# Attention scores in two-bank PSUM tiles, with one tanh and one exp for two heads

## The chip, the cores and the metric

The kernel runs on one core of one Trainium2 chip. The metric is the device time of one execution in microseconds (us), as the median of several runs. The five engines are TensorE (PE, with its weight loads as PEld), VectorE (DVE), ScalarE (ACT), GpSimd (POOL) and SyncE (SP), which issues most of the transfers. PSUM, into which TensorE writes, has eight banks of 512 float32 values per partition.

## What is computed

The reference is attention with capped scores, followed by a layer norm, a feed-forward block and a residual:

```python
scores = (1 / np.sqrt(64)) * np.matmul(q, k.transpose(0, 1, 3, 2))   # batch 4, 12 heads, 448 tokens, 64 wide
scores = cap * np.tanh(scores / cap)                                 # cap = 30
scores = scores - np.max(scores, axis=-1, keepdims=True)
attn = np.exp(scores)
attn = attn / (np.sum(attn, axis=-1, keepdims=True) + 1e-09)
x = np.matmul(attn, v)             # heads joined to (4, 448, 768)
xn = (x - mean) / np.sqrt(var + 1e-06) * g_ln
out = x + np.maximum(xn @ w_ch1, 0.0) @ w_ch2                        # 768 -> 3072 -> 768
```

All is float32; w_ch1 and w_ch2 arrive as float64. Since tanh bounds the scores by the cap, the kernel leaves out the maximum and lets the exponent's sums run as they are. (A second program for other caps, `general`, lies beside it and does not run here.)

## The kernel before

There are 48 heads (4 batches of 12). They are worked in quads: four heads, as two pairs p = 0, 1, with k = 0, 1 for the head of a pair. Keys are cut into three blocks of 128 (j = 0, 1, 2) and a leftover of 64. For a pair and a block, TensorE multiplies keys with queries for both heads (line 639; the two heads sit on the two halves of the partitions and are issued alternately), into two tiles of one PSUM bank each. ScalarE evacuates each bank with a tanh of 448 elements (line 684) into the tile `e`, and after three blocks raises a head's 3 x 448 values with one exp (line 688). The leftover keys of the quad's four heads share two more banks (line 666), two tanh and one exp of 2 x 448 (line 696). Then TensorE multiplies with v (line 480, leftover line 487) into two output banks `o`; VectorE adds up the key blocks (lines 503 and 505), TensorE sums them over partitions (lines 562 and 566) into one bank `s`; outputs and sums are copied out of PSUM (lines 535 and 537), transposed (lines 588 and 602, banks `f`) and divided (line 612).

Beside this, while heads 0 to 23 run, VectorE and GpSimd convert the first weights from float64 (lines 859 to 867, split in two at lines 420 and 423), and layer norms of the first token tiles follow (lines 769 to 819). The feed-forward block in two parts fills the rest of the time: lines 930 to 964 first, with the remaining heads spread between, and from about 500 us lines 1139 to 1231 for the other token tiles.

The order of all this is not written by hand. Each operation is added with an engine, a cost in ns and a due time; `Order.emit` plays a list scheduler over these costs, and each engine's queue gets its instructions in the order in which that scheduler started them. On the chip each queue runs in that order and waits where it must. A place in PSUM is handed out by the scheduler: kind `bank` has eight places, and a tag has a limit of its own (`zf`, the scores of heads 0 to 23, six banks; `z`, later scores, four; `o` two; `s` one; `f` six). A place that comes free goes to the end of the list and the first of the list is taken. `fits` refuses an operation whose places aren't free, and the scheduler goes on to the next operation by due time. `realize` makes one tile per bank. Names that the steps touch: `quad` (line 433 chooses `zf` or `z`), `products` (the score matmuls), `scores` with `into` (tanh and exp), `TAGS`, `Order.add`, `Order.emit`, `realize`.

Of the kernel before, what the change touches and what calls it, by code (L numbers as in the profile page):

```python
# [32 lines left out]
WRAP = 4  # L33
LEAD = 24
SPLIT = 28
SLOTS = 8
# [56 lines left out]
TAGS = dict(  # L93
    z=('bank', 4), zf=('bank', 6), o=('bank', 2), s=('bank', 1), f=('bank', 6), kq=('d', 4), v=('v', 3), s1=('d', 2), er=('d', 2),
    e=('e', 3), e2=('e', 2), kh=('k', 2), kl=('k', 2), ot=('b', 4), ss=('b', 1), stage=('a', 3),
# [14 lines left out]
class Buf:  # L110


    def __init__(self, pool, kind, tag, shape, dtype):
        self.pool, self.kind, self.tag, self.shape, self.dtype = pool, kind, tag, shape, dtype
        self.users, self.ap, self.last, self.share, self.since = 0, None, 0.0, None, 0.0


# [19 lines left out]
class Order:  # L137
# [4 lines left out]
    def __init__(self, places, limits):  # L142
        self.places, self.limits = places, limits
        self.ops, self.writer, self.readers, self.taken, self.dead = [], {}, {}, [], set()

    def add(self, engines, fn, reads=(), writes=(), allocs=(), due=0.0, dma=0, after=(), lag=0.0):
# [29 lines left out]

    def emit(self, realize):
        free = {e: 0.0 for e in "SGVATP"}
# [15 lines left out]
        def fits(o):  # L194
            if o.wait and not slots[o.wait[0]] and o.wait[1].ap is None:
                return False
            need = {}
            for b in o.bufs:
                if b.ap is None:
                    for k in keys(b):  # L200
                        need[k] = n = need.get(k, 0) + 1
                        if len(slots[k]) < n:
                            o.wait = k, b
                            return False
            return True

        while pending:
            done = False
            for e in free:
# [25 lines left out]
                for b in o.bufs:  # L235
                    b.users -= 1
                    b.last = max(b.last, o.end)
                    if b.share:
                        b.share.last = max(b.share.last, b.last)
                        b.share.users -= not b.users  # L240
                        if not b.users and not b.share.users:
                            for at in b.share.at:
                                heappush(due_back, (b.share.last + CROSS, *at))
                    elif not b.users:
                        for k, at in zip(keys(b), b.at):
                            heappush(due_back, (b.last + CROSS, k, at))
# [99 lines left out]
class Program:  # L346
    def __init__(self, tc, general, ahead, kq, v, w1, w2, out):
# [8 lines left out]
        self.order = Order(self.places, self.limits)  # L356
        self.given, self.grown = {}, {}
        if not general:
# [33 lines left out]
    def realize(self, b, at):  # L392
        key = (b.pool, b.kind, at)
        if key not in self.tiles:
            self.tiles[key] = self.pools[self.grown.get(key, b.pool)].tile([128, self.sizes[b.pool, b.kind]], F32, bufs=1, name=f"{b.kind}{at}")
# [9 lines left out]
        return ap  # L405

    def eng(self, e):
# [18 lines left out]
    def quad(self, i, at):  # L426
# [5 lines left out]

        self.zs = "zf" if i < FIRST else "z"
        kqs = []
# [138 lines left out]
    def finish(self, i, pairs, ps, due, late):  # L573
# [23 lines left out]
        for j, tl, p in self.token_tiles(b):  # L597
# [17 lines left out]
            if tl >= NA:  # L615
# [4 lines left out]
                    reads=writes, writes=[("xd", tl, (h0, p.start))], due=due, dma=128 * W * 4)  # L620

    def products(self, kqs, l, r, due, into, allocs, at_once):

# [18 lines left out]
        for n in range(0, len(slots), at_once):  # L642
            now = slots[n:n + at_once]
            zs = [[self.buf("ps", self.zs, [128, 512], F32) for _ in range(2)] for _ in now]

            def qk(e, now=now, zs=zs):
                for (p, j), z in zip(now, zs):
                    for both in zip(*(mul(z[k].ap[:, :S], p, k, j) for k in range(2))):
                        for one in both:
                            one()  # L650
# [3 lines left out]
            self.add({"T": 200 + len(now) * cost}, qk, reads=[x for p in ps for x in sources(p)],  # L654
                     writes=[z for zz in zs for z in zz], allocs=[allocs[p] for p in ps], due=due[now[0][0]] - PLAN["qk"])
            for (p, j), z in zip(now, zs):
                for k in range(2):
                    into(p, k, j, z[k])

        def rest(cost=0, then=None, reads=(), writes=()):  # L660
            zs = [self.buf("ps", self.zs, [128, 512], F32) for _ in range(2)]

            def qk(e):
                for p, kq in enumerate(kqs):
                    for k, z in enumerate(zs):
                        self.nc.tensor.matmul(z.ap[p * REST:p * REST + REST, :S], lhsT=kq.ap[rows[k], l, 128 * NK:],
                                              rhs=kq.ap[rows[k], r], start=True, stop=True)
# [5 lines left out]
            for k, z in enumerate(zs):  # L673
                into(2, k, 0, z)

        return rest

    def scores(self, es, er, kqs, due, at_once):
        nc, add = self.nc, self.add
        tiles = [*es, er]  # L680
        parts = lambda p, k: [(tiles[p], k, j) for j in range(NK if p < 2 else 1)]
# [12 lines left out]
        def finish(*a):  # L694
            rest(*a)
            add({"A": ACTS(2 * S) + 93}, lambda e: nc.scalar.activation(er.ap, er.ap, AF.Exp, scale=self.capt),
                reads=parts(2, 0) + parts(2, 1), writes=[er], due=due[2])

        return finish

    def scores_general(self, es, er, kqs, due, at_once):
# [6 lines left out]

        def into(p, k, j, z):
            add({"A": ACTP(S) + 93}, lambda e: nc.scalar.activation(  # L710
                tiles[p].ap[:, k, j] if p < 2 else tr.ap[:, k], z.ap[:, :S], AF.Tanh, scale=self.sc),
                reads=[z], writes=[tiles[p]], due=due[p])

# [601 lines left out]

    def close(self, *names):
        for n in names:
            self.cms.pop(n).__exit__(None, None, None)
# [4 lines left out]
    def run(self):  # L1323
# [13 lines left out]
        self.open("xna", side="right")  # L1337
        self.open("ps", 1, PSUM)

        A0, ASTEP, BSTEP = PLAN["start"], PLAN["step"], PLAN["bstep"]  # L1340
# [58 lines left out]
        self.planned = self.order.emit(self.realize)  # L1399
        self.close("ps", "wd", "hc", "xo2", "xo1", "y", "xC", "xd", "small")  # L1400
# [53 lines left out]
```

## Time and profile before

| | |
|---|---|
| median of 3 runs | 872.41 us (872.37 to 874.22) |
| the profiled execution, own time | 872.27 us |
| its span, first to last instruction | 870.5 us |
| granted TensorE clock, mean | 0.997 |
| PE busy | 850.3 us (98%) |
| DVE busy | 701.3 us (81%) |
| ACT busy | 523.8 us (60%) |
| POOL busy | 162.4 us (19%) |

The profile is one execution, and 1.8 us of its time lie outside the span. Busy times are unions of an engine's records. Matmul records are pipelined and each float32 matmul shows as two records, so a mean per record is longer than its share of the queue; where a duration matters, it is better read from one start to the next. "issue" in the chain of waits is time in which an engine waited for nothing that the profile shows. The wide picture of the span in 40 slices is of little use here, since a slice is 22 us long; tables by stage are of more.

### The profile page before, as it was taken

How to read it: one execution, taken by the hardware profiler on the slowest of the kernel's cores; microseconds unless marked ns; L12 is line 12 of the kernel's file. 1: busy time of each engine (PE TensorE's matmuls, PEld its weight loads, DVE VectorE, ACT ScalarE, POOL GpSimd, SP SyncE). 2: the span in 40 equal slices, each digit the busy share in tenths (PEclk: the TensorE clock that was granted, in tenths of full speed). 3: DMA queues.
4: the chain of work that ended last, by engine and by line, in shares of the span. 5: the costliest groups of instructions: out<-in, count | busy, mean ns of one | idle time of the engine just before them, and what ended most of it. 6: DMA issues, size and time to landing. Idle time of an engine off the chain costs nothing.

```text
span 870.5 us, 12961 instructions
## 1 busy us (share of the span) xinstructions
PE 850.3 (98%) x4718; PEld 705.6 (81%) x4718; DVE 701.3 (81%) x1154; ACT 523.8 (60%) x860; POOL 162.4 (19%) x206
## 2 busy tenths in 40 slices
PE   8899999999999999999999999999999999999995
PEld 4344477979889799799799988989998999898984
DVE  2996597888789779687689978887888788878884
ACT  7889848645654646445436545665666566656750
POOL 1430041211122111111110002223122312231121
PEclk9999999999999999999999999999999999999998
DMA  9996527566676675654563245787879787968697
GB/s 233 237 265 169 140 69 228 164 216 172 181 218 194 198 211 158 192 177 114 179 237 110 73 164 109 162 164 142 181 157 174 132 182 161 177 124 186 129 180 188
DMA packets 55003, 148.97 MB, mean 171 GB/s; under 512 B 7312, under 2 KB 19088, under 8 KB 54928
## 3 DMA queue, kind: packets, MB, share of 16 engines
q1 hardware_dynamic: 41680, 111.86, 43.1%
q0 software_dynamic: 13248, 36.18, 25.0%
q8 instruction: 39, 0.64, 0.3%
q14 instruction: 36, 0.29, 0.1%
HBM read 85.88 MB, written 62.13 MB: 170 GB/s over the span
## 4 chain that ended last, share of the span: by engine, by line
PE 86%; DVE 5%; DMA 2%; ACT 2%; issue 1%; POOL 1%; SPq 0%; DVEq 0%; POOLq 0%
PE bank L1139 7%; PE bank L1142 7%; PE bank L1140 7%; PE bank L1219 6%; PE bank L1221 6%; PE bank L1220 6%; PE bank L959 6%; PE bank L930 6%; PE bank L961 5%; PE bank L960 5%; PE bank L932 5%; PE bank L931 5%; PE bank L480 5%; PE bank L639 4%; PE bank L602 1%; PE bank L562 1%
## 5 line engine op out<-in xcount | busy, mean ns | idle before, releaser
L1236 POOL DMA_DIRECT2D out_dram<-x x92 | 80.5, 1000 | 333.1 <-ACT x L1227 209.1
L1227 ACT ACTIVATE x<-bank 128x384 f32<-128x384 f32 x184 | 87.6, 488 | 38.7 <-PE bank L1221 32.4
L1139 PE MATMUL bank<-X,q 128*128 128x512 f32 x252 | 100.0, 397 | 2.0 <-ACT y L1151 1.9
L1231 DVE TENSOR_TENSOR x<-bank,x 128x384 f32<-128x384 f32 x141 | 75.9, 553 | 30.8 <-PE bank L1221 24.5
L930 PE MATMUL bank<-hA,q 128*128 128x384 f32 x288 | 100.1, 348 | 0.1
L684 ACT ACTIVATE e<-bank,sc 128x448 f32<-128x448 f32 x144 | 81.7, 666 | 30.4 <-PE bank L639 30.2
L1140 PE MATMUL bank<-X,q 128*128 128x512 f32 x252 | 99.5, 395 | 0.0
L1142 PE MATMUL bank<-X,q 128*128 128x512 f32 x252 | 99.4, 395 | 0.0
L959 PE MATMUL bank<-w,hh 128*128 128x384 f32 x288 | 98.4, 342 | 0.0
L1219 PE MATMUL bank<-w,hop 128*128 128x384 f32 x288 | 97.4, 338 | 0.6 <-DVE x L1231 0.3
L932 PE MATMUL bank<-hA,q 128*128 128x384 f32 x288 | 97.6, 339 | 0.3 <-DVE q L423 0.3
L931 PE MATMUL bank<-lA,q 128*128 128x384 f32 x288 | 97.5, 338 | 0.0
L961 PE MATMUL bank<-w,hl 128*128 128x384 f32 x288 | 97.2, 338 | 0.0
L960 PE MATMUL bank<-w,hh 128*128 128x384 f32 x288 | 97.2, 337 | 0.0
L1221 PE MATMUL bank<-w,hop 128*128 128x384 f32 x288 | 96.9, 337 | 0.0
L1220 PE MATMUL bank<-w,hop 128*128 128x384 f32 x288 | 96.8, 336 | 0.0
L862 POOL TENSOR_SCALAR raw<-raw 128x768 f32<-128x768 f32 x48 | 54.5, 1138 | 225.5 <-ACT c L858 209.2
L964 DVE TENSOR_TENSOR x<-bank,x 128x384 f32<-128x384 f32 x144 | 75.7, 547 | 11.7 <-PE bank L961 11.3
L688 ACT ACTIVATE e<-e,capt 128x1344 f32<-128x1344 f32 x48 | 66.6, 1456 | 0.0
L480 PE MATMUL bank<-e,v 128*64 128x448 f32 x288 | 60.7, 547 | 1.9 <-ACT d L684 1.0
L930 PEld LDWEIGHTS bank<-hA,q 128*128 128x128 f32 x288 | 54.0, 188 | 9.0 <-issue 5.5
L416 ACT ACTIVATE w<-c 128x768 fp32r<-128x768 f32 x33 | 27.9, 845 | 54.5 <-DVE c L867 23.6
(162 smaller groups left out, 1823.5 us busy)
## 6 DMA issues: line engine op xcount, KB each, us to landing
raw<-in_w_dram SPq DMA_DIRECT2D x48, 768.0 KB, 5.1
out_dram<-x POOLq DMA_DIRECT2D x92, 384.0 KB, 7.4
kept<-c SPq DMA_DIRECT2D x47, 384.0 KB, 5.6
d<-in_kq_dram SPq DMA_DIRECT2D x48, 224.0 KB, 6.3
d<-kept SPq DMA_DIRECT2D x24, 384.0 KB, 5.1
c<-kept SPq DMA_DIRECT2D x23, 384.0 KB, 3.5
v<-in_v_dram SPq DMA_DIRECT2D x24, 227.5 KB, 5.7
v<-in_v_dram SPq DMA_DIRECT2D x24, 195.0 KB, 6.0
```

The lines of the kernel that those rows point to most:

```text
L930: nc.tensor.matmul(ps.ap[:, :n], lhsT=w1h.ap[:, wc], rhs=xh.ap[:, c], start=(c == 0), stop=False)
L931: nc.tensor.matmul(ps.ap[:, :n], lhsT=w1h.ap[:, wc], rhs=xl.ap[:, c], start=False, stop=False)
L932: nc.tensor.matmul(ps.ap[:, :n], lhsT=w1l.ap[:, wc], rhs=xh.ap[:, c], start=False, stop=(c == CC - 1))
L959: nc.tensor.matmul(o, lhsT=h[0].ap[:, mc], rhs=w[0].ap[:, hc], start=(f == 0), stop=False)
L960: nc.tensor.matmul(o, lhsT=h[0].ap[:, mc], rhs=w[1].ap[:, hc], start=False, stop=False)
L961: nc.tensor.matmul(o, lhsT=h[1].ap[:, mc], rhs=w[0].ap[:, hc], start=False, stop=(f == last))
L1139: nc.tensor.matmul(ps.ap, lhsT=wh.ap[:, wc], rhs=xs[c].ap[:, 0], start=start and c == 0, **o)
L1140: nc.tensor.matmul(ps.ap, lhsT=wh.ap[:, wc], rhs=xs[c].ap[:, 1], start=False, **o)
L1142: nc.tensor.matmul(ps.ap, lhsT=wl.ap[:, wc], rhs=xs[c].ap[:, 0], start=False, **o)
L1219: nc.tensor.matmul(o, lhsT=hh.ap[:, mc], rhs=wh.ap, start=start, stop=False, **skip)
L1220: nc.tensor.matmul(o, lhsT=hh.ap[:, mc], rhs=wl.ap, start=False, stop=False, **skip)
L1221: nc.tensor.matmul(o, lhsT=hl.ap[:, mc], rhs=wh.ap, start=False, stop=True, **skip)
```

## The change

Four aligned two-bank tiles are made at the start and cover PSUM. Everything that took one bank takes a half of such a tile. The scores of heads 0 to 23 take a whole one: the two heads of a pair (or the two banks of leftover keys) stand in its two halves, one tanh reads both (2 x 448 elements), and one exp raises the two heads' 2 x 3 x 448 values. The costs given to the scheduler are 1000 for such a tanh and twice the former cost for such an exp. Heads 24 to 47 keep single banks, tanh of 448 and exp of 1344.

The scheduler's `take` gives a wide buffer a pair of places that are both free, and gives a single bank, as long as wide buffers are still to come, first a place whose partner is taken. Since one tile now has two banks whose users have nothing to do with one another, `emitted` declares for each instruction on PE, DVE and ACT that it needs no order against the last 40 accesses of the tile's other bank by another engine, unless they share something else, or the instruction touches a tile for the first time after a pool was closed.

```diff
+PAST = 40
+TANH, EXP = 1000, ACTS(NK * S) + 93
-    z=('bank', 4), zf=('bank', 6), o=('bank', 2), s=('bank', 1), f=('bank', 6), ...
+    z=('bank', 4), zf=('bank', 3), o=('bank', 2), s=('bank', 1), f=('bank', 6), ...
...
         for b in op.bufs:
+            self.wide += b.wide and not b.users
...
+    def take(self, slots, b, kind):
+
+        if kind != "bank":
+            return [slots.pop(0)] if slots else None
+        if b.wide:
+            at = next((at for at in slots if not at % 2 and at + 1 in slots), None)
+            if at is None:
+                return None
+            slots.remove(at)
+            slots.remove(at + 1)
+            return [at, at + 1]
+        if not slots:
+            return None
+        at = min(slots, key=lambda at: (at ^ 1 in slots and self.wide > 0, slots.index(at)))
+        slots.remove(at)
+        return [at]
...
-                        need[k] = n = need.get(k, 0) + 1
-                        if len(slots[k]) < n:
+                        if k not in left:
+                            left[k] = list(slots[k])
+                        if not self.take(left[k], b, None if k[0] else k[2]):
                             o.wait = k, b
...
-                        b.at = [slots[k].pop(0) for k in keys(b)]
-                        b.ap = realize(b, b.at[0])
-                o.fn(e)
+                        b.at = [(k, at) for k in keys(b) for at in self.take(slots[k], b, None if k[0] else k[2])]
+                        b.ap = realize(b, b.at[0][1])
+                        self.wide -= b.wide
+                run(o, e)
...
+        if b.kind == "bank":
+            two = self.tiles["ps", "two", at // 2]
+            if b.wide:
+                return two.rearrange("p (k n) -> p k n", k=2)[:, :, :S]
+            self.tiles[key] = two[:, at % 2 * 512:at % 2 * 512 + 512]
...
+    def emitted(self, op, e):
...
+        for x in block.instructions[n:]:
+            reads, writes = (list(self.regions(side)) for side in (x.ins, x.outs))
+            names = {t for t, _, _ in reads + writes}
+            fresh = self.reused and names - self.seen
+            self.seen |= names
+            banks = {(t, k) for t, lo, hi in reads + writes if t in self.pairs for k in range(2) if lo < 512 * k + 512 and hi > 512 * k}
+            for t, k in banks:
+                other = t, 1 - k
+                if other not in banks and not fresh:
+                    for y, before, after in self.recent.get(other, ()):
+                        if x.engine != y.engine and not (meet(writes, before + after) or meet(reads, after)):
+                            self.tc.declare_no_dep(x, y, reason="another bank of the tile")
+                past = self.recent.setdefault((t, k), [])
+                past.append((x, reads, writes))
+                del past[:-PAST]
...
+    def scored(self):
+        if self.zs == "z":
+            return [self.buf("ps", "z", [128, 512], F32) for _ in range(2)]
+        z = self.buf("ps", "zf", [128, 2, 512], F32)
+        z.wide = True
+        return [z]
...
-        def into(p, k, j, z):
-            add({"A": ACTP(S) + 93}, lambda e: nc.scalar.activation(
-                tiles[p].ap[:, k, j] if p < 2 else er.ap[:, k], z.ap[:, :S], AF.Tanh, scale=self.sc),
-                reads=[z], writes=[(tiles[p], k, j)], due=due[p])
-            if p < 2 and j == NK - 1:
-                add({"A": ACTS(NK * S) + 93}, lambda e: nc.scalar.activation(
-                    tiles[p].ap[:, k], tiles[p].ap[:, k], AF.Exp, scale=self.capt),
-                    reads=parts(p, k), writes=[(tiles[p], k)], due=due[p])
+        both = slice(0, 2)
+
+        def into(p, j, zs):
+            for k, z, ks in [(k, z, [k]) for k, z in enumerate(zs)] if len(zs) == 2 else [(both, *zs, [0, 1])]:
+                add({"A": TANH if len(ks) == 2 else ACTP(S) + 93}, lambda e, k=k, z=z: nc.scalar.activation(
+                    tiles[p].ap[:, k, j] if p < 2 else er.ap[:, k], z.ap if len(z.shape) > 2 else z.ap[:, :S], AF.Tanh, scale=self.sc),
+                    reads=[z], writes=[(tiles[p], x, j) for x in ks], due=due[p])
+                if p < 2 and j == NK - 1:
+                    add({"A": EXP * len(ks)}, lambda e, k=k: nc.scalar.activation(
+                        tiles[p].ap[:, k], tiles[p].ap[:, k], AF.Exp, scale=self.capt),
+                        reads=[(tiles[p], x, j) for j in range(NK) for x in ks], writes=[(tiles[p], x) for x in ks], due=due[p])
...
     def close(self, *names):
+        self.reused = True
...
+        for i in range(4):
+            self.tiles["ps", "two", i] = self.pools["ps"].tile([128, 1024], F32, bufs=1, name=f"two{i}")
```

## Rows read from the trace of the kernel before

**Rows 1.** Busy us, share of the span and instructions of three engines.
```profile
PE 850.3 (98%) x4718; PEld 705.6 (81%) x4718; DVE 701.3 (81%) x1154; ACT 523.8 (60%) x860; POOL 162.4 (19%) x206
```

**Rows 2.** Busy us by stage; columns in the first line.
```profile
core 0: us, PE busy (x) PEld busy (x) DVE busy (x) ACT busy (x) POOL busy (x), PEclk, DMA share, GB/s
0.00:10.00 10.00, 8.70 (x41) 6.91 (x42) 1.35 (x11) 4.89 (x9) 1.50 (x15) 1.00 0.75 162
0.00:110.00 110.00, 103.18 (x611) 44.89 (x612) 73.94 (x139) 94.35 (x138) 22.62 (x50) 1.00 0.79 209
200.00:300.00 100.00, 100.00 (x590) 88.70 (x590) 82.04 (x124) 57.51 (x81) 18.45 (x17) 1.00 0.64 187
30.00:40.00 10.00, 8.82 (x44) 2.94 (x44) 9.97 (x17) 8.02 (x12) 2.75 (x4) 1.00 1.05 279
12.00:32.00 20.00, 17.18 (x101) 6.53 (x102) 13.59 (x16) 19.81 (x29) 5.69 (x8) 1.00 0.93 261
62.00:74.00 12.00, 10.99 (x72) 5.08 (x70) 8.19 (x20) 11.81 (x17) 0.88 (x1) 1.00 1.00 270
74.00:106.00 32.00, 31.42 (x204) 11.92 (x200) 18.89 (x36) 29.04 (x47) 1.02 (x7) 1.00 0.46 121
```

**Rows 3.** The chain of waits, 12 to 107 us: start us, us, what.
```profile
12.16 7.29 DMA raw<-in_w_dram
...
35.04 1.46 DVE d L503
...
62.20 1.14 ACT e L684 x2
...
68.46 2.63 ACT e L684 x5
...
72.22 1.47 ACT e L688
...
74.19 0.63 DVE lA L819
...
106.18 1.15 ACT e L684 x2
```

**Rows 4.** Waits, 10 to 110 us: us in total, times, longest us.
```profile
ACT e L684 <- PE bank L639: 7.8, 7, 2.1
...
PEld bank L480 <- ACT e L688: 3.6, 4, 1.3
```

**Rows 5.** The tanh group, 0 to 130 us: busy us, mean ns, idle before.
```profile
L684 ACT ACTIVATE e<-bank,sc 128x448 f32<-128x448 f32 x82 | 46.7, 688 | 12.1 <-PE bank L639 12.1
```

**Rows 6.** ScalarE in order of time, 70 to 90 us: start us, us.
```profile
70.91 2.77 ACT L688 ACTIVATE e<-e,capt 128x1344 f32<-128x1344 f32 x2
73.53 3.00 ACT L815 ACTIVATE hA<-bank,gt 128x384 fp32r<-128x384 f32 x6
...
77.58 3.39 ACT L684 ACTIVATE e<-bank,sc 128x448 f32<-128x448 f32 x6
80.68 2.90 ACT L688 ACTIVATE e<-e,capt 128x1344 f32<-128x1344 f32 x2
...
85.48 1.05 ACT L696 ACTIVATE d<-d,capt 128x896 f32<-128x896 f32 x1
86.41 2.75 ACT L684 ACTIVATE e<-bank,sc 128x448 f32<-128x448 f32 x5
```

**Rows 7.** All engines in order of time, 24 to 28 us: start us, us.
```profile
24.18 2.53 PE L639 MATMUL bank<-d 64*128 64x448 f32 x12
...
25.71 3.39 ACT L684 ACTIVATE e<-bank,sc 128x448 f32<-128x448 f32 x6
...
27.59 1.14 DVE L537 COPY b<-bank 128x448 f32<-128x448 f32 x2
```

More of the change, by code (lines that the diff above doesn't have):

```diff
@@ L93 @@
 TAGS = dict(
-    z=('bank', 4), zf=('bank', 6), o=('bank', 2), s=('bank', 1), f=('bank', 6), kq=('d', 4), v=('v', 3), s1=('d', 2), er=('d', 2),
+    z=('bank', 4), zf=('bank', 3), o=('bank', 2), s=('bank', 1), f=('bank', 6), kq=('d', 4), v=('v', 3), s1=('d', 2), er=('d', 2),
     e=('e', 3), e2=('e', 2), kh=('k', 2), kl=('k', 2), ot=('b', 4), ss=('b', 1), stage=('a', 3),
@@ L115, in __init__ @@
         self.users, self.ap, self.last, self.share, self.since = 0, None, 0.0, None, 0.0
+        self.wide, self.at = False, ()
 class Part:
@@ L144, in __init__ @@
         self.ops, self.writer, self.readers, self.taken, self.dead = [], {}, {}, [], set()
+        self.wide = 0
     def add(self, engines, fn, reads=(), writes=(), allocs=(), due=0.0, dma=0, after=(), lag=0.0):
@@ L175, in drop, with emit @@
             self.slots[kind].remove(at)
-    def emit(self, realize):
+    def take(self, slots, b, kind):
[13 more added lines that the diff above has]
+        return [at]
+    def emit(self, realize, run):
         free = {e: 0.0 for e in "SGVATP"}
@@ L196, in fits @@
                 return False
-            need = {}
+            left = {}
             for b in o.bufs:
@@ L244, in emit @@
                     elif not b.users:
-                        for k, at in zip(keys(b), b.at):
+                        for k, at in b.at:
                             heappush(due_back, (b.last + CROSS, k, at))
@@ L356, in __init__ @@
         self.order = Order(self.places, self.limits)
-        self.given, self.grown = {}, {}
+        self.given, self.grown, self.seen, self.recent, self.reused = {}, {}, set(), {}, False
         if not general:
@@ L405, in realize, with regions @@
         return ap
+    def regions(self, side):
+        for a in side:
+            ap = getattr(a, "bass_ap", None)
+            if ap is not None:
+                (pitch, _), *dims = ap.ap
+                lo = ap.offset % pitch
+                yield ap.tensor.name, lo, lo + 1 + sum(d * (n - 1) for d, n in dims)
+    def emitted(self, op, e):
+        block = self.nc.cur_bb.bb
+        n = len(block.instructions)
+        op.fn(e)
+        if self.general or e not in "TVA":
+            return
+        meet = lambda one, two: any(a[0] == b[0] and a[1] < b[2] and b[1] < a[2] for a in one for b in two)
+        for x in block.instructions[n:]:
[13 more added lines that the diff above has]
+                del past[:-PAST]
     def eng(self, e):
@@ L431, in quad @@
         part = HEADS[i // H]
-        self.zs = "zf" if i < FIRST else "z"
+        self.zs = "zf" if i < FIRST and not self.general else "z"
         kqs = []
@@ L620, in finish, with score @@
                     reads=writes, writes=[("xd", tl, (h0, p.start))], due=due, dma=128 * W * 4)
+    def scored(self):
[4 more added lines that the diff above has]
+        return [z]
+    def score(self, z, k):
+        return z[0].ap[:, k, :S] if len(z) == 1 else z[k].ap[:, :S]
     def products(self, kqs, l, r, due, into, allocs, at_once):
@@ L643, in products @@
             now = slots[n:n + at_once]
-            zs = [[self.buf("ps", self.zs, [128, 512], F32) for _ in range(2)] for _ in now]
+            zs = [self.scored() for _ in now]
             def qk(e, now=now, zs=zs):
                 for (p, j), z in zip(now, zs):
-                    for both in zip(*(mul(z[k].ap[:, :S], p, k, j) for k in range(2))):
+                    for both in zip(*(mul(self.score(z, k), p, k, j) for k in range(2))):
                         for one in both:
@@ L654, in products @@
             self.add({"T": 200 + len(now) * cost}, qk, reads=[x for p in ps for x in sources(p)],
-                     writes=[z for zz in zs for z in zz], allocs=[allocs[p] for p in ps], due=due[now[0][0]] - PLAN["qk"])
+                     writes=[b for z in zs for b in z], allocs=[allocs[p] for p in ps], due=due[now[0][0]] - PLAN["qk"])
             for (p, j), z in zip(now, zs):
-                for k in range(2):
-                    into(p, k, j, z[k])
+                into(p, j, z)
         def rest(cost=0, then=None, reads=(), writes=()):
-            zs = [self.buf("ps", self.zs, [128, 512], F32) for _ in range(2)]
+            zs = self.scored()
             def qk(e):
                 for p, kq in enumerate(kqs):
-                    for k, z in enumerate(zs):
-                        self.nc.tensor.matmul(z.ap[p * REST:p * REST + REST, :S], lhsT=kq.ap[rows[k], l, 128 * NK:],
+                    for k in range(2):
+                        self.nc.tensor.matmul(self.score(zs, k)[p * REST:p * REST + REST], lhsT=kq.ap[rows[k], l, 128 * NK:],
                                               rhs=kq.ap[rows[k], r], start=True, stop=True)
@@ L672, in rest @@
                      writes=[*zs, *writes], allocs=[allocs[2]], due=due[2] - PLAN["qk"])
-            for k, z in enumerate(zs):
-                into(2, k, 0, z)
+            into(2, 0, zs)
         return rest
@@ L696, in finish @@
             add({"A": ACTS(2 * S) + 93}, lambda e: nc.scalar.activation(er.ap, er.ap, AF.Exp, scale=self.capt),
-                reads=parts(2, 0) + parts(2, 1), writes=[er], due=due[2])
+                reads=[(er, k, 0) for k in range(2)], writes=[er], due=due[2])
         return finish
@@ L707, in scores_general, with into @@
         ms = [self.buf("small", "m", [128, 2 * NK], F32, 4) for _ in range(3)]
[L709 to L712, printed above, removed]
+        def into(p, j, zs):
+            for k, z in enumerate(zs):
+                add({"A": ACTP(S) + 93}, lambda e, k=k, z=z: nc.scalar.activation(
+                    tiles[p].ap[:, k, j] if p < 2 else tr.ap[:, k], z.ap[:, :S], AF.Tanh, scale=self.sc),
+                    reads=[z], writes=[tiles[p]], due=due[p])
         self.products(kqs, 1, 0, due, into, tiles, at_once)()
@@ L1338, in run @@
         self.open("ps", 1, PSUM)
+        for i in range(4):
+            self.tiles["ps", "two", i] = self.pools["ps"].tile([128, 1024], F32, bufs=1, name=f"two{i}")
+        self.pairs = {self.tiles["ps", "two", i].tensor.name for i in range(4)}
         A0, ASTEP, BSTEP = PLAN["start"], PLAN["step"], PLAN["bstep"]
@@ L1398, in run @@
                     o.left += 1
-        self.planned = self.order.emit(self.realize)
+        self.planned = self.order.emit(self.realize, self.emitted)
         self.close("ps", "wd", "hc", "xo2", "xo1", "y", "xC", "xd", "small")
```

1 line of the change is left out of this document (removed).

## The prediction

> **What bounds the kernel now.** I read the busy shares first. TensorE is busy 98% of the span, VectorE 81%, ScalarE 60% [rows 1]. Such means hide stages, so the busy time by stage comes next. From 200 to 300 us TensorE is busy 100.00 of 100 us: nothing that shortens ScalarE can gain there. In the first 110 us it is busy 103.18 us and idle 6.82 [rows 2]; the first 10 us of start-up hold 1.30 of that (8.70 busy of 10.00) [rows 2], so that about 5.5 us lie in the stretch of heads 0 to 23, which is the stretch the change touches. That is the first cap on what can come back.
>
> Who holds TensorE up inside this stretch changes along the way. From 12 to 32 us ScalarE is busy 19.81 of 20 us and TensorE loses 2.82; from 62 to 74 us ScalarE is busy 11.81 of 12 and TensorE loses 1.01; from 74 to 106 us TensorE loses only 0.58 of 32 and sets the pace itself; and from 30 to 40 us VectorE is full (9.97 of 10) while ScalarE has two us of room [rows 2]. The chain of waits says the same in another way: its pieces from 12.16 to 36.50 us are transfers, weight conversions on GpSimd and VectorE and VectorE's adds (24 pieces, of which the first and the last stand in the rows; none is ScalarE's), while ScalarE's tanh and exp stand on it from 62.20 to 73.69 [rows 3]. The waits by name say something that the chain does not: the weight loads of the product with v waited 3.6 us for the exp of line 688 [rows 4].
>
> **The change part by part.** *Instructions.* The program has six quads in heads 0 to 23. A quad now issues twelve tanh for the two pairs of heads and two for the leftover keys, all of 448 elements, and four exp of 1344. After the change there are seven tanh of 896 and two exp of 2688. So 84 tanh become 42 and 24 exp become 12.
>
> *What one is worth.* A record's own mean (688 ns for a tanh) [rows 5] is no price, since records of a queue overlap. Starts are: six tanh from 77.58 to 80.68 are 0.517 us each; two exp from 70.91 to 73.53 are 1.31 each; the exp of 896 elements runs from 85.48 to 86.41, 0.93 [rows 6]. From 896 to 1344 elements an exp grows by 0.38 us, so 448 elements cost 0.38 and the rest, about 0.14, is what each instruction costs for itself. A tanh of 896 then takes 0.517 + 0.38 = 0.90 (upper bound 0.93, the exp of that size), against 1.03 for two: 0.14 saved, at least 0.10. An exp of 2688 takes 1.31 + 3 x 0.38 = 2.45, against 2.62: 0.17 saved. No row has an instruction that reads two banks or one of 2688 elements; I take the line through the three sizes, since it passes through neighbours of the same engine. The sum is 42 x 0.14 + 12 x 0.17 = 7.9 us of ScalarE (6.2 with the lower bound for the tanh). The Trainium skill, ScalarE: Activation LUTs, section What ACT_TABLE_LOAD costs, gives an ACTIVATE with a pointer operand some 280 ns beside its elements, of which back-to-back ones overlap by 93; by it each merge saves about 0.19 us, and the 54 of them 10.1 us, an estimate; the trace's smaller 0.14 is what I use.
>
> *What of it reaches the end.* From 12 to 32 us ten tanh pairs and three exp pairs run: 10 x 0.14 + 3 x 0.17 = 1.9 us. The chain gives none of it to ScalarE, and VectorE is full right behind, so the lower bound is 0; the waits of the v product for exp speak for more. I take the middle, 1.0. From 62 to 74 us the chain has ten tanh (first and last piece in the rows) and four exp, two of them in pieces called issue: 5 x 0.14 + 2 x 0.17 = 1.0 us, and TensorE's 1.01 us of idle there just covers it; I take 1.0, bounds 0.5 and 1.0, since the next piece on the chain is VectorE's work for the norm, line 819 [rows 3], which may be late of itself. From 74 to 106 us TensorE is the bound: 0, at most its 0.58. At 106.18 one more tanh pair is on the chain [rows 3]: 0.1. Together 2.1 us; bounds 0.6 and 3.6.
>
> *Latency.* One tanh now waits for the matmuls of both heads. They are issued alternately and end together, so this costs nothing; if it did not hold, it would cost a slot's half, 0.4 us, where ScalarE had run dry. Both the v product and the first add of line 503 already wait for the exps of both heads, so the joint exp delays nobody.
>
> *Banks.* Score space was up to six single banks and becomes up to three aligned pairs. Outputs (two banks), sums (one) and transposes take single banks of the same eight, placed where the partner is already taken. While the two outputs and the sum are held, two pairs are left. A pair comes back when its one tanh ends, 0.90 us after its start, where the first single bank came back after 0.52. TensorE's matmul that waits for it stands at the head of its queue, and behind it the products with v, the sums and the transposes, whose readers are VectorE and ScalarE. The Trainium skill, PSUM — Partial Sum Buffer, section PSUM bank collisions raise a hardware error, wants any two engines kept apart per bank; no run here shows the price of more than that, and the pair is such a case, being held whole for one reader. Price, from a place where three slots were written at once: they begin at 24.18 and take 2.53, so the third begins near 25.86, when the first tanh has only just begun, at 25.71, and the last copies out of the outputs begin at 27.59 [rows 7]. With two pairs the third slot waits till 25.71 + 0.90 = 26.61, that is 0.75 us. The written order is made with the pairs in it and can put other matmuls there, so I take 0; the bounds are 0 and 12 (two per quad) x 0.75 = 9 us.
>
> *Order.* The list scheduler writes all queues from costs. A tanh pair is now 1000 in place of 2 x 561, a joint exp 2 x 1443 as before, so queues of VectorE, GpSimd and the DMA issues on SyncE are reordered a little, without new instructions. I count 0, with 1 us either way: after 110 us TensorE is full and its work is the same. Between the banks of one tile a false order would make a matmul wait for a neighbour's evacuation; the declarations take these away for the last 40 accesses of a bank, and leave them only for instructions that touch a tile for the first time once pools have been closed. These are evacuations by ScalarE and VectorE, which have room [rows 1]: 0, bound 1 us.
>
> *Sum.* The profiled execution took 872.27 us (span 870.5), the median of three is 872.41; the two agree within 0.14. 872.27 - 2.1 = 870.2. The wider tanh are worth 7.9 us to ScalarE and about a quarter of that to the kernel.
>
> **The rivals.** *All of TensorE's idle time comes back.* For it: ScalarE is full just where TensorE loses most. Against: the chain from 12 to 35 us names transfers and VectorE. It gives 872.27 - 5.5 = 866.8.
>
> *The gain is off the path.* VectorE stays late with its weight conversions (full from 30 to 40 us [rows 2]), and what ScalarE finds early at 62 us it waits for again: ScalarE already waited 7.8 us for score matmuls [rows 4]. Then only the last pieces count, some 0.3 us: 872.0.
>
> *Pairs run short.* This ends slower. The 0.75 us of the bank price fall on TensorE at half of the twelve places, 6 x 0.75 = 4.5 us, less the 2.1 gained: 872.27 + 2.4 = 874.7. For it: score banks were filled six deep beside held outputs [rows 7]. Against: ScalarE, the engine that is full, reads a pair faster than two singles, and TensorE's queue has other work in most places. It decides once more than three of the twelve places wait in earnest (3 x 0.75 = 2.2).
>
> *The change doesn't do what it says*: order between the banks stays in force, so that matmuls wait for neighbours. It would show through the whole program, not in its first 110 us; I see no reason in the diff and count it into the slower case.
>
> **How the numbers follow.** A measurement of this kernel can tell about 0.2%, here 1.7 us, from no change; so faster means below 870.7 and slower above 874.2. The forecast, 868.7 to 871.7 by its bounds, has 0.45, of which 0.35 lie below 870.7 and 0.10 within; all idle back 0.13; off the path 0.24, within; pairs short 0.18, slower. That makes faster 0.48, same 0.34, slower 0.18. The range reaches from the full return, 866.8, to 874.0, which leaves out most of the slower case and a little below the full return: 2 in 10 at most.
>
> **What would show it.** Right: tanh of 896 that start 0.88 to 0.93 us apart, exp of 2688 some 2.45 apart, ScalarE's busy time in the first 110 us down by 6 to 8 us, TensorE's idle from 12 to 32 and 62 to 74 us down by about 2 us in all, and TensorE still full from 200 us on. The first price is wrong if two banks in one instruction cost extra; the path step is wrong if TensorE's idle is the same and VectorE ends its waits; the bank step is wrong if score matmuls wait for tanh of line 684 more than now. A difference that arises after 200 us would mean that the order, not the instruction, made it, and that I cannot derive from these rows.

## The result and the profile after

| | median us (lowest to highest) | against the kernel before |
|---|---|---|
| before, measured beside it | 873.18 (872.37 to 874.22), 5 runs | |
| after | 878.72 (876.57 to 879.82), 5 runs | 1.0062, 95% interval 1.0044 to 1.0080 |

The change makes the kernel slower by 0.6%, some 5.5 us. The forecast was 870.2 us with a range up to 874.0, so it was wrong in sign and the time lies above the range. The profiled execution of after took 879.58 us, its span is 877.8.

Where the time went is plain from one event that both traces have: the last sums over partitions (line 566 before, 628 after) of heads 20 to 23. First the kernel before, then the one after, TensorE in order of time (start us, us):

```profile
102.74 0.94 PE L566 MATMUL bank<-d,ones 128*32 128x448 f32 x8
```

```profile
109.56 0.94 PE L628 MATMUL two<-d,ones 128*32 128x448 f32 x8
```

The delay is 6.8 us there, and the whole span is longer by 7.3. So most of the loss arises in the stretch of heads 0 to 23, where the changed instructions stand. Up to the end of this event, before and then after:

```profile
core 0: us, PE busy (x) PEld busy (x) DVE busy (x) ACT busy (x) POOL busy (x), PEclk, DMA share, GB/s
0.00:103.68 103.68, 96.86 (x576) 40.91 (x579) 70.06 (x124) 89.80 (x130) 22.23 (x47) 1.00 0.80 212
```

```profile
0.00:110.50 110.50, 101.08 (x580) 43.49 (x584) 68.94 (x124) 83.90 (x78) 21.28 (x47) 0.97 0.74 199
```

TensorE is idle for 9.42 us in place of 6.82, so 2.6 of the 6.8 us are waits. It has four more matmul records behind it (580 against 576), by their lines one score slot of the next quad, about 1 us of work that only comes earlier. And its granted clock is lower for a while, which is priced below at 2.75 us. After by stage (columns as above), to be held against [rows 2]:

```profile
0.00:110.00 110.00, 100.58 (x576) 43.41 (x576) 68.94 (x124) 83.90 (x78) 21.28 (x47) 0.97 0.74 199
12.00:32.00 20.00, 15.57 (x93) 6.01 (x94) 13.95 (x15) 18.62 (x15) 6.28 (x8) 1.00 0.86 252
30.00:40.00 10.00, 8.45 (x26) 2.98 (x20) 9.72 (x17) 4.69 (x5) 2.62 (x4) 0.66 1.05 272
200.00:300.00 100.00, 100.00 (x601) 87.94 (x598) 79.76 (x127) 58.65 (x85) 18.42 (x20) 1.00 0.67 197
```

From 200 us on TensorE is full as before. From 12 to 32 us it now loses 4.43 us in place of 2.82. And from 30 to 40 us two things show that the kernel before did not have: ScalarE works 4.69 us of 10 in place of 8.02, and TensorE's granted clock is 0.66. What ScalarE waits for is in the waits of after from 10 to 110 us (us in total, times, longest us):

```profile
ACT e L755 <- PE two L711: 17.6, 10, 3.8
```

ScalarE's wait for score matmuls was 7.8 us [rows 4] and is 17.6. Not all of that is loss: the work that ScalarE is spared (89.80 us busy before the event, now 83.90) also turns up as waiting. What tells more is how long TensorE itself stands before score matmuls until VectorE has read a bank (waits of TensorE, 10 to 110 us). Before, then after:

```profile
PE bank L666 <- DVE r L591: 0.9, 1, 0.9
...
PE bank L639 <- DVE x L612: 0.4, 1, 0.4
```

```profile
PE two L711 <- DVE x L674: 1.6, 2, 1.1
PE two L711 <- DVE b L599: 1.3, 1, 1.3
PE two L711 <- DVE r L653: 1.0, 1, 1.0
```

It was 1.3 us and is 3.9, which is as much more as TensorE's idle time has grown. VectorE's instructions named here are the copies out of outputs and sums (b) and the reads of transposes (r and x). Here is one such place, after, all engines in order of time; it is the place of [rows 7]:

```profile
24.31 1.90 ACT L755 ACTIVATE e<-two,sc 128x896 f32<-128x896 f32 x2
25.64 0.61 DVE L599 COPY b<-two 128x448 f32<-128x448 f32 x1
26.31 1.02 PE L711 MATMUL two<-d 64*128 64x448 f32 x4 [1.32 <-DVE b L599]
27.38 1.01 ACT L755 ACTIVATE e<-two,sc 128x896 f32<-128x896 f32 x1 [1.17 <-PE two L711]
...
31.65 1.02 PE L711 MATMUL two<-d 64*128 64x448 f32 x2 [1.01 <-DVE r L653]
33.21 3.35 PE L711 MATMUL two<-d 64*128 64x448 f32 x6 [0.54 <-DVE x L674]
35.11 1.01 ACT L755 ACTIVATE e<-two,sc 128x896 f32<-128x896 f32 x1 [3.25 <-PE two L711]
36.49 4.21 PE L542 MATMUL two<-e,v 128*64 128x448 f32 x12
```

Before, three score slots were written in one go at 24.18. Now the third waits at the head of TensorE's queue for the copy of the sums, whose bank is half of its pair, and ScalarE then stands idle for 1.17 us. At 31.65 and 33.21 the two halves of one pair are held by two banks of transposes: two records go when r has been read and the others only after x. (The kernel before waited there too, 0.93 us for r and 0.36 for x; the waits are not new, but now one slot needs both.) ScalarE stands idle for 3.25 us. After these waits the records run at half the clock: the granted clock is 0.60 from 33 to 34 us and 0.50 from 34 to 40, and the twelve of the product with v take 4.21 us, where they take 2.48 at the full one.

The five runs of after differ in this. The run with a mean granted clock of 0.997, which is that of the profiled execution before, took 876.57 us; the four with 0.993 to 0.995 took 877.94 to 879.82. So some 4 us of the loss (876.57 against 872.27) are there at an equal clock, and the rest goes with a lower one.

The instructions themselves are as priced. ScalarE alone, after:

```profile
6.96 3.70 ACT L755 ACTIVATE e<-two,sc 128x896 f32<-128x896 f32 x4 [1.89 <-PE two L711]
10.54 2.55 ACT L759 ACTIVATE e<-e,capt 128x2688 f32<-128x2688 f32 x1
12.96 1.92 ACT L755 ACTIVATE e<-two,sc 128x896 f32<-128x896 f32 x2
```

Four joint tanh from 6.96 to 10.54 are 0.895 us each (0.90 was the estimate), and the joint exp takes 2.42 (2.45).

### The profile page after: what moved, and what is told of

Same layout as the page of the kernel before. It is cut to its first block, busy times and chain, and to the rows that moved or that the text cites. A ratio compares the mean times of both kernels' runs of the same rounds, so it can differ in the third digit from the quotient of the medians.

```text
span 877.8 us, 12875 instructions
## 1 busy us (share of the span) xinstructions
PE 854.1 (97%) x4718; PEld 708.1 (81%) x4718; DVE 699.3 (80%) x1154; ACT 516.5 (59%) x806; POOL 163.1 (19%) x206
## 4 chain that ended last, share of the span: by engine, by line
PE 86%; DVE 5%; DMA 3%; issue 2%; ACT 1%; POOL 1%; SPq 0%; DVEq 0%; POOLq 0%
PE two L1211 7%; PE two L1214 6%; PE two L1212 6%; PE two L1291 6%; PE two L1293 6%; PE two L1292 6%; PE two L1031 6%; PE two L1002 6%; PE two L1032 5%; PE two L1033 5%; PE two L542 5%; PE two L1004 5%; PE two L1003 5%; PE two L711 5%; PE two L624 1%
## 5 line engine op out<-in xcount | busy, mean ns | idle before, releaser
L1299 ACT ACTIVATE x<-two 128x384 f32<-128x384 f32 x184 | 87.5, 488 | 39.9 <-PE two L1293 32.3
L1211 PE MATMUL two<-X,q 128*128 128x512 f32 x252 | 100.1, 397 | 2.0 <-ACT y L1223 1.9
L755 ACT ACTIVATE e<-two,sc 128x448 f32<-128x448 f32 (+1 forms) x108 | 75.3, 763 | 43.8 <-PE two L711 43.8
L1002 PE MATMUL two<-hA,q 128*128 128x384 f32 x288 | 100.1, 348 | 0.0
L1303 DVE TENSOR_TENSOR x<-two,x 128x384 f32<-128x384 f32 x141 | 75.8, 553 | 30.3 <-PE two L1293 24.2
L1212 PE MATMUL two<-X,q 128*128 128x512 f32 x252 | 99.5, 395 | 0.0
L1214 PE MATMUL two<-X,q 128*128 128x512 f32 x252 | 99.5, 395 | 0.0
L1291 PE MATMUL two<-w,hop 128*128 128x384 f32 x288 | 97.5, 339 | 1.1 <-DVE c L1303 0.6
L1031 PE MATMUL two<-w,hh 128*128 128x384 f32 x288 | 98.5, 342 | 0.0
L1004 PE MATMUL two<-hA,q 128*128 128x384 f32 x288 | 97.6, 339 | 0.3 <-DVE q L485 0.3
L1003 PE MATMUL two<-lA,q 128*128 128x384 f32 x288 | 97.5, 339 | 0.0
L1033 PE MATMUL two<-w,hl 128*128 128x384 f32 x288 | 97.3, 338 | 0.0
L1032 PE MATMUL two<-w,hh 128*128 128x384 f32 x288 | 97.3, 338 | 0.0
L1293 PE MATMUL two<-w,hop 128*128 128x384 f32 x288 | 96.9, 337 | 0.0
L1292 PE MATMUL two<-w,hop 128*128 128x384 f32 x288 | 96.9, 336 | 0.0
L1036 DVE TENSOR_TENSOR x<-two,x 128x384 f32<-128x384 f32 x144 | 75.8, 546 | 12.0 <-PE two L1033 11.6
L759 ACT ACTIVATE e<-e,capt 128x1344 f32<-128x1344 f32 (+1 forms) x36 | 63.6, 1795 | 0.3
```

What stands on the lines that cost most here:

```text
L1002: nc.tensor.matmul(ps.ap[:, :n], lhsT=w1h.ap[:, wc], rhs=xh.ap[:, c], start=(c == 0), stop=False)
L1003: nc.tensor.matmul(ps.ap[:, :n], lhsT=w1h.ap[:, wc], rhs=xl.ap[:, c], start=False, stop=False)
L1004: nc.tensor.matmul(ps.ap[:, :n], lhsT=w1l.ap[:, wc], rhs=xh.ap[:, c], start=False, stop=(c == CC - 1))
L1031: nc.tensor.matmul(o, lhsT=h[0].ap[:, mc], rhs=w[0].ap[:, hc], start=(f == 0), stop=False)
L1032: nc.tensor.matmul(o, lhsT=h[0].ap[:, mc], rhs=w[1].ap[:, hc], start=False, stop=False)
L1033: nc.tensor.matmul(o, lhsT=h[1].ap[:, mc], rhs=w[0].ap[:, hc], start=False, stop=(f == last))
```

## The experiments

The theory after the result: **pairs run short**. A score slot needs an aligned pair, halves of which are held by outputs, sums and transposes; fewer slots are written ahead, ScalarE runs dry, and TensorE, which waits in order, stands too. Rivals: order left between the banks of a tile; the joint instructions; the order that the scheduler writes from the new costs. All medians below are beside runs of the kernel before on the same chip (872.5 to 873.2).

| run | median us | ratio to before, 95% interval | ScalarE's wait for score matmuls, 10 to 110 us |
|---|---|---|---|
| before | | | 7.8 |
| after | 878.72 | 1.0062 (1.0044 to 1.0080) | 17.6 |
| two-bank tiles alone | 872.90 | 1.0000 (0.9988 to 1.0012) | 8.0 |
| pairs, narrow instructions | 880.06 | 1.0071 (1.0055 to 1.0087) | 11.0 |
| any neighbouring banks | 876.06 | 1.0038 (1.0025 to 1.0052) | 15.1 |
| joint exp on the kernel before | 875.01 | 1.0022 (1.0011 to 1.0033) | 9.3 |
| pairs, joint tanh, two exp | 877.69 | 1.0063 (1.0045 to 1.0081) | 13.7 |
| neighbours, joint tanh, two exp | 877.52 | 1.0058 (1.0041 to 1.0076) | 13.9 |
| before with four score banks | 881.40 | 1.0094 (1.0074 to 1.0113) | 20.1 |
| before with five score banks | 882.24 | 1.0107 (1.0088 to 1.0126) | 19.6 |
| after with two pairs | 877.71 | 1.0057 (1.0041 to 1.0072) | 17.9 |
| after, transposes in one bank | 877.46 | 1.0055 (1.0037 to 1.0073) | 14.5 |
| after, costs as measured | 878.91 | 1.0068 (1.0055 to 1.0082) | 10.9 |
| pairs in the first quad alone | 874.43 | 1.0013 (1.0004 to 1.0022) | 9.1 |
| the same with two exp | 875.09 | 1.0032 (1.0021 to 1.0043) | 9.2 |
| before, lighter exp | 871.56 | 0.9983 (0.9974 to 0.9992) | 9.7 |

The last column, from one profiled execution each, does not follow the time: it is 11.0 us for pairs with narrow instructions, which are slower than after with 17.6, and it grows to 9.7 with the lighter exp, which is faster than before. So ScalarE running dry does not by itself explain the loss.

**Tiles without pairs.**

```diff
-    zf=('bank', 3)
+    zf=('bank', 6)
...
-        z = self.buf("ps", "zf", [128, 2, 512], F32)
-        z.wide = True
-        return [z]
+        return [self.buf("ps", self.zs, [128, 512], F32) for _ in range(2)]
```

> Edit: the two-bank tiles and the declared order stay, but the scores of heads 0 to 23 take single banks again (limit six) with one tanh of 448 per bank and one exp of 1344 per head, so each queue holds the same operations in the same order as before. Pairs run short (my theory): 872.5 to 874, as before, since nothing has to be a pair. Order between banks of a tile costs time (rival): 876 or more, as the changed kernel. Joint instructions or the written order (rivals): as before too.

872.90, ratio 1.0000. ScalarE's wait is that of before (waits, 10 to 110 us):

```profile
ACT e L751 <- PE two L707: 8.0, 7, 2.1
```

Order between the banks costs nothing here; that rival falls.

**Pairs without joint instructions.**

```diff
+            for k in range(2):
+                z = zs[-1] if len(zs) == 1 else zs[k]
+                add({"A": ACTP(S) + 93}, ... self.score(zs, k), AF.Tanh ..., reads=[z], writes=[(tiles[p], k, j)])
...
```

> Edit: scores keep their aligned pairs, but each half is read by a tanh of its own (448 elements) and each head has an exp of its own; the scheduler's costs are the former ones. Pairs run short: the same shortage without the saving, 878 to 882. Joint instructions cause the loss (rival: a long tanh or exp holds up those behind it): 872.5 to 874. The scheduler's new costs cause it (rival): 872.5 to 874.

880.06: the pairs alone cost 0.7%, with the old instructions and the old costs. The joint instructions as the only cause fall, and so do the new costs. The run with a granted clock of 0.997 took 878.81 us, so most of this stands without a lower clock. But the path is not the one of after. TensorE's score matmuls here wait for VectorE for only 0.3 us in all, and at the place shown above three slots are again written in one go (waits, then TensorE in order of time):

```profile
PE two L711 <- DVE x L674: 0.3, 1, 0.3
```

```profile
24.88 2.53 PE L711 MATMUL two<-d 64*128 64x448 f32 x12
...
111.06 0.94 PE L628 MATMUL two<-d,ones 128*32 128x448 f32 x8
```

The last sums still come at 111.06. So that pairs cost is shown; that they cost by TensorE's waits for held halves is seen in after alone. The order that the scheduler writes around too few pairs is the other way in which they can cost, and no run separates the two.

**Pairs of any neighbours.**

```diff
-            at = next((at for at in slots if not at % 2 and at + 1 in slots), None)
+            at = next((at for at in slots if at + 1 in slots), None)
...
```

> Edit: one eight-bank tile in place of four two-bank ones; a score pair may be any two neighbouring free banks (seven places in place of four), single banks go first where fewest neighbours are free; joint tanh and exp as in the changed kernel. Pairs run short by alignment: most of the 6 us come back, 871 to 875. Joint instructions or the scheduler's costs (rivals): 877 to 880.

876.06: with seven places for a pair in place of four, by the medians a part of the loss comes back, not most of it; the expectation was too bold. The interval (1.0025 to 1.0052) just overlaps that of the changed kernel (from 1.0044). ScalarE's wait is still 15.1 us.

**The joint exp on the kernel before.**

```diff
-            if p < 2 and j == NK - 1:
+            if p < 2 and j == NK - 1 and (k or self.zs == "z"):
+                ks = [k] if self.zs == "z" else [0, 1]
...
```

> Edit on the kernel before: one exp of 2688 for two heads in place of two of 1344 for heads 0 to 23, single banks and tanh of 448 as before. By the rows 12 x 0.17 = 2.0 us of ScalarE are saved. If joint instructions are harmless: 870.5 to 873.5. If the joint exp's length holds up what is behind it (rival): 875 or more.

875.01, slower by 0.2% where 2 us of ScalarE are saved. The first product with v shows where; ScalarE and TensorE before, then with the joint exp:

```profile
9.71 2.75 ACT L688 ACTIVATE e<-e,capt 128x1344 f32<-128x1344 f32 x2
11.21 0.97 PE L480 MATMUL bank<-e,v 128*64 128x448 f32 x2 [0.60 <-ACT e L688]
12.51 2.47 PE L480 MATMUL bank<-e,v 128*64 128x448 f32 x10 [0.34 <-ACT e L688]
```

```profile
10.84 2.57 ACT L690 ACTIVATE e<-e,capt 128x2688 f32<-128x2688 f32 x1
13.47 4.17 PE L480 MATMUL bank<-e,v 128*64 128x448 f32 x12 [2.44 <-ACT e L690]
```

Before, the matmul for the first head starts after that head's exp, at 11.21. With the joint exp all wait until 13.47, TensorE is idle for 2.44 us in one piece, and then runs at half the clock (4.17 us for twelve records). Product and exp belong together per head, whatever the scheduler's own dependencies say.

**Two exp in the changed kernel.**

```diff
-                    add({"A": EXP * len(ks)}, ... tiles[p].ap[:, k] ..., writes=[(tiles[p], x) for x in ks])
+                for x in ks if p < 2 and j == NK - 1 else ():
+                    add({"A": EXP}, ... tiles[p].ap[:, x] ..., writes=[(tiles[p], x)])
```

> Edit on the changed kernel: aligned pairs and one tanh of 896 stay, but each head has its own exp of 1344 again; the order written for TensorE and VectorE is unchanged. Joint exp holds up the first product with v and lets TensorE's clock fall: 875 to 877.5, some 1 to 3 us less than the changed kernel. Shortage of pairs alone (rival): 878 to 881, since ScalarE loses 2 us of saving and nothing else changes.

877.69: between the two expectations and by the medians not told apart from the changed kernel, so beside the pairs the joint exp seems of little weight; that is not shown. The profiled execution is of use for something else, since TensorE's and VectorE's orders are the same as after:

```profile
26.21 1.02 PE L711 MATMUL two<-d 64*128 64x448 f32 x4 [0.33 <-DVE b L599]
...
31.55 1.02 PE L711 MATMUL two<-d 64*128 64x448 f32 x2 [0.99 <-DVE r L653]
33.10 2.33 PE L711 MATMUL two<-d 64*128 64x448 f32 x6 [0.54 <-DVE x L674]
35.36 2.48 PE L542 MATMUL two<-e,v 128*64 128x448 f32 x12
```

The waits for r and x are there as after, the one for b is 0.33 us in place of 1.32, and the clock stayed at its upper level (2.4 GHz; granted 1.00 from 0 to 110 us): from the six score records to the end of the product 4.74 us (33.10 to 37.84), where after takes 7.49 (33.21 to 40.70). By this comparison the lower level (1.2 GHz) cost that execution of after 2.75 us. The Trainium skill, TensorE: Matmul & The Clock Gate, section Part 1: The HAM clock gate, says of a kernel's start that the number of matmuls run at the lower level varies from run to run of one kernel. No trace here compares two starts of one kernel; what the runs of after show is that their mean granted clock varies, from 0.993 to 0.997.

**Neighbours with two exp.** The two edits together.

> Edit: any two neighbouring banks of one eight-bank tile for a score pair, one tanh of 896, but an exp of 1344 for each head. Shortage of aligned pairs and the joint exp are both causes: 871 to 874.5, at or a little under the kernel before. If the joint tanh itself or the larger score tiles cost as much (rival): 875 to 877, as with the joint exp.

877.52, a miss: no better than neighbours with the joint exp. The single effects do not add up, and neither makes a joint tanh pay. It also weakens the run with any neighbours: that alignment is a part of the loss is not shown.

**How many score banks.** First the kernel before with four, later with five in place of six, and the changed kernel with two pairs in place of three.

```diff
-    zf=('bank', 6)
+    zf=('bank', 4)
```

> Edit on the kernel before: single banks, but at most four of them for the scores of heads 0 to 23, in place of six, as many as two pairs hold. If the number of score banks is what the pairs take away: 875 to 879. If it is that both halves come back together and that transposes break the pairs (rival): 872 to 874.

> Edit on the kernel before: at most five single banks for the scores of heads 0 to 23, between the six of the kernel before and the four that cost some 9 us. If the price follows the number of banks: 874 to 879. If only the step below five hurts, so that pairs that can use five of eight banks would be free (rival): 872 to 873.5.

> Edit on the changed kernel: at most two pairs for the scores in place of three. If a third pair is of no use because its halves are held by outputs, sums and transposes: 877 to 881, as the changed kernel. If the third pair is used and the loss comes from each wait for a whole joint tanh (rival): 883 or more, as the kernel before lost some 9 us with four single banks.

881.40, 882.24 and 877.71. The first two are above every range that was expected. The price is not gradual: five banks cost as much as four. A slot takes two banks, so either holds two slots, and only six hold three. The changed kernel is not told apart with two pairs from what it is with three: the third pair brings nothing that these runs show. With five banks the start shows the mechanism; ScalarE before, then ScalarE and TensorE with five banks, in order of time:

```profile
12.32 3.29 ACT L684 ACTIVATE e<-bank,sc 128x448 f32<-128x448 f32 x6
```

```profile
12.24 2.24 ACT L684 ACTIVATE e<-bank,sc 128x448 f32<-128x448 f32 x4
12.43 2.47 PE L480 MATMUL bank<-e,v 128*64 128x448 f32 x10 [0.34 <-ACT e L688]
14.83 1.02 PE L639 MATMUL bank<-d 64*128 64x448 f32 x4
15.89 1.16 ACT L684 ACTIVATE e<-bank,sc 128x448 f32<-128x448 f32 x2 [1.40 <-PE bank L639]
...
35.39 1.16 ACT L684 ACTIVATE e<-bank,sc 128x448 f32<-128x448 f32 x2 [4.06 <-PE bank L639]
```

Before, six tanh ran through at 12.32; here the last slot of the quad is written only after the product with v, and ScalarE waits.

**Transposes in one bank.**

```diff
+    ft=('bank', 1)
...
-        pr = buf("ps", "f", [128, 512], F32)
+        turned = "ft" if i < FIRST else "f"
+        pr = buf("ps", turned, [128, 512], F32)
```

> Edit on the changed kernel: the transposes of heads 0 to 23 take turns in one bank in place of up to six, so that they share a tile with the sums and two whole tiles stay for scores. If transposes that hold halves make pairs short: 873 to 877. If what is lost is lost to the outputs and the sums, or turns in one bank queue up (rival): 878 to 883.

877.46, between the two expectations and not told apart from after: inconclusive.

**Costs as measured.**

```diff
-TANH, EXP = 1000, ACTS(NK * S) + 93
+TANH, EXP = 900, 1215
```

> Edit on the changed kernel: the scheduler's costs are set to what the trace shows, 900 for a joint tanh and 1215 per head for an exp, in place of 1000 and 1423; instructions and banks are unchanged, the order differs. If the written order suffered from wrong costs (rival): 873 to 876. If the shortage of pairs is what costs: 877 to 881, as the changed kernel.

878.91, as the changed kernel: an order written from wrong costs as the cause falls a second time.

**Pairs in the first quad alone.**

```diff
+        self.first = i == 0 and not self.general
...
+        if not self.first:
+            return [self.buf("ps", "zf", [128, 512], F32) for _ in range(2)]
...
```

> Edit on the changed kernel: only heads 0 to 3 take pairs, joint tanh and joint exp; heads 4 to 23 take single banks (limit six), a tanh of 448 per bank and an exp per head. At the first quad no output, sum or transpose holds a bank yet. If pairs cost only where banks are held by others: 871 to 874, at most 1.3 us gained (7 x 0.14 + 2 x 0.17). If pairs cost wherever they stand: 874 or more.

> Edit: as the run with pairs for heads 0 to 3 alone, but with an exp for each head. If the joint exp's first wait of TensorE matters (2.4 us in one piece): 0.5 to 2 us under the run with the joint exp in the first quad, 870.5 to 873. If it doesn't: 0.3 us more than that run.

874.43 and 875.09: even where no other user holds a bank yet, nothing is gained. Two exp are not better there, so of the second run's two cases the one in which the joint exp does not matter is the nearer. Why a quad of free pairs still loses 1 to 2 us stays open; pairs held by others are not the reason, so shortage in this sense is not the whole cost of pairs. One part may be the start, where a joint tanh waits for both heads' matmuls; ScalarE before, then with pairs in the first quad:

```profile
6.60 3.26 ACT L684 ACTIVATE e<-bank,sc 128x448 f32<-128x448 f32 x6 [1.52 <-PE bank L639]
```

```profile
7.35 3.70 ACT L758 ACTIVATE e<-two,sc 128x896 f32<-128x896 f32 x4 [2.32 <-PE two L714]
```

**What ScalarE's time is worth.**

```diff
+                n = S if self.zs == "z" else 316
...
-                    tiles[p].ap[:, k], tiles[p].ap[:, k], AF.Exp, scale=self.capt),
+                    tiles[p].ap[:, k, :, :n], tiles[p].ap[:, k, :, :n], AF.Exp, scale=self.capt),
```

> Edit on the kernel before: for heads 0 to 23 each exp covers 316 of 448 columns per key block (the other columns keep their tanh, so this part of the computation is left out). 24 x 396 elements x 0.84 ns = 8.0 us less of ScalarE, as much as the joint instructions were to save; order, banks and waits are those of the kernel before. If ScalarE's time is worth about a quarter at the end (my sum): 869.5 to 871.5, so 1 to 3 us under the kernel before. If it is worth nothing (rival): 872 to 873.5. If all of TensorE's idle time was ScalarE's (rival): 866 to 868.

871.56, ratio 0.9983 (0.9974 to 0.9992): about 8 us less of ScalarE, with the order and banks of before, are worth 1.5 us (0.7 to 2.3 by the interval). ScalarE's wait for score matmuls grows from 7.8 to 9.7 us.

## Why the prediction was wrong, by its own steps

- *What one instruction is worth*: right. 0.895 and 2.42 us measured, 0.90 and 2.45 estimated. Reading two banks in one instruction costs nothing extra in these rows.
- *What of it reaches the end*: right in size. The step said 2.1 us of 7.9, bounds 0.6 and 3.6; the lighter exp shows 1.5 of about 8. Where in the stretch it comes back was not compared.
- *Latency*: the tanh begins 0.36 us later where ScalarE has nothing to do yet (6.96 after, 6.60 before), close to the 0.4 us that the step named and did not count. It failed for the exp. The step said that the product with v already waits for both heads' exps. That is how the scheduler's operations depend; on the chip each matmul waits for the head it reads, as the 11.21 row shows. By itself the joint exp costs 0.2% on the kernel before.
- *Banks*: failed, and this is the step that decided. It took 0 within bounds of 0 and 9 us, arguing that the written order can put other matmuls there. Pairs alone cost 0.7% (about 6 us), and fewer whole slots on the kernel before 0.9 to 1.1%. The step priced one place at 0.75 us and named the tanh as what frees the pair; the trace shows 1.32 us, freed by VectorE's copy, and the prediction had itself read VectorE as full from 30 to 40 us. In after a pair is held by whoever holds its other half. How the 6 us come about when the instructions are narrow, where such waits are 0.3 us, stays open.
- *Order*: right where it said 0. Two-bank tiles with the declared order cost nothing, and costs as measured change nothing that can be told apart. What the scheduler writes differently because pairs are few belongs to the step on banks, and was not tested alone.
- *The rivals*: the one on pairs had the shortage and the sign, with 874.7 us; after is 878.72. Its gross term, 4.5 us, should have been some 7.5, an estimate: 5.5 lost net, plus the 2 that ScalarE's saving was to give. A fall of TensorE's clock after its waits was in no step; in the profiled execution it makes 2.75 us.
- *Chances and range*: 0.18 for slower was too little, given that the price of the banks had bounds up to 9 us and was entered with its lower end. A bound four times as large as the forecast gain has to weigh in the middle value.

## What to carry to other kernels

Buffers written ahead of a busy engine come in whole slots: count how many slots fit beside everything else that holds the memory, before and after, and price the loss of one with a run that only lowers the limit, before building anything. Joining two buffers for one longer instruction ties each half to the fate of the other, and its users on a busy engine can then set the pace. Eight us saved on an engine that is full for most of a stretch brought 1.5 here, so little is needed to eat them up.

## What was not expected of the hardware

One slot fewer is dear: from six score banks to five the kernel before loses 9 us. And waits can cost TensorE twice: after waits of 1.32, 0.77, 1.01 and 0.54 us between 25 and 33 us it ran at 1.2 GHz from about 33.2 to 40 us in one execution. In another kernel with the same orders, where the first of them was 0.33 us and the others as long within 0.02, it did not. Which of its waits let the clock fall was not settled.
